# A convolution head and a state-space head on one core: 31 tasks of a written order put elsewhere

## The chip, the cores and the metric

The kernel runs on one core of one Trainium2 chip. The metric is the device time of one execution in microseconds. The median of three runs of the kernel before is 351.68 us (350.0 to 353.27).

## The reference

Two independent computations over 2048 time steps and 1024 channels are put side by side in the output. Inputs and output are bfloat16.

```python
# part A: a gated long convolution
k_shift = sum_t k_pad[:, t:t+S] * shift_k[:, ks-1-t]        # 4 taps along time
kv = k_shift * v
y = irfft(rfft(kv, 2S) * rfft(ssm_k, 2S))[:S]               # per channel, along time
a = q * (y + kv * ssm_D)
# part B: a diagonal complex state-space layer
Lam_bar = exp(dt * Lam);  B_bar = ((Lam_bar - 1) / Lam)[:, None] * Bmat
h_t = Lam_bar * h_{t-1} + x_t @ B_bar.T                     # for t in 0..2047
b = 2 * real(h @ Cmat.T) + x * Dskip
out = concatenate([a, b], -1)
```

## The kernel before, in words

Part A does its transform of length 4096 as 128 times 32 with matmuls. Three arrays in DRAM carry it from stage to stage: `Ys_kv` (first stage of kv), `Ys_h` (first stage of the filter) and `Vs` (after the product). Part B goes over 16 chunks of 128 time steps; a real rotation before and after lets the vector engine's scan do the complex recurrence.

Nothing is scheduled by the machine. The string `ORDER` lists 1489 tasks, and the program calls them in that order (`manual_schedule`, line 766). Each engine and each issuing queue runs its own instructions strictly in that order, and an instruction that waits holds up all that stand behind it on its engine. A task is written `name.arguments:slots`. Slots are chosen by hand: `a` a unit of the on-chip arena of 53 units (2 KB per partition each), `p` one of 8 PSUM banks, `w` one of three slots for transform weights, `h` one of three slots for a chunk's state. A slot that is still in use makes the task wait.

The tasks that matter here, by engine:

- SP issues loads, and a DMA that waits blocks the queue: `x.i` (line 447) a transposing load of chunk i of x, 256 KB; `lh.i` and `lk.i` (676) 512 KB from `Ys_h` and `Ys_kv`, i from 0 to 15; `lw.i` (671) 160 KB of transform weights; `swp.i.q` (707) an exchange on the chip, 256 KB, which copies the even or odd partitions of a tile to the others; `vl.n` (741) 512 KB from `Vs`; `qp.r` (746) 512 KB of q; `osp`, `ysp`, `ysh` stores of the output. `kp.r` (570 to 573) loads rows of k into a ring of eight.
- POOL issues `sw.i.q`, the same exchange from its own queue; `vst.i` (736), 512 KB to `Vs`; `yst.i` (563), `ost.r` (763) stores of the output; `ld_G` (398) a constant.
- PE: `U.i.*` (464), chunk i times B; `yq.i.k` and `y.i.*` (538; 520 and 523), chunk i times C; `sh.g` and `sk.g` (687), second transform stage of filter and kv for group g, two groups to each i; `sa.g` (725), the inverse stage; `a3.n.*` (753), the last stage.
- ACT empties the banks: `ue` (473), `ye` (556), `she` (696), `ske` (703), `sae` (733), `a3e` (760). A `v` at the end of the name (`uev`, `shev`, `a3ev`) puts the same copy on DVE.
- DVE: `r1`, `r2`, `sc`, `r3`, `r4` (487, 498, 504, 510), rotation, scan and rotation of a chunk; `pr.i` (713), the product of the two spectra, which needs both exchanges of i and the evictions of both groups; `qm.r` (762), the gate with q.

So pair i goes: `lw`, `lh`, `lk`, then `sh`/`sk` on PE, `she`/`ske` on ACT, `sw`/`swp`, `pr` on DVE, `sa` on PE, `sae`, `vst`. All sixteen `vst` must land before the first `vl`. The last stage then runs to the end beside the last chunks of part B.

Of the kernel before, what the change touches and what calls it, by code (L numbers as in the profile page):

```python
# [133 lines left out]
sae.1.1:a40 sae.0.0 lw.5:w1 sae.0.1 vst.3 yq.6.4 sh.10:p0p2 yq.6.5 sw.2.0 sh.11:p3p5 yq.6.6 x.14:a36 swp.2.1 sae.1.0  # L134
she.10.1:a0 she.11.1 yq.6.7 sk.4:p1p4 yq.7.0:p5p2 she.10.0 r1.8:a6 ye.6.0:a37 ske.4.0 ye.6.1 ske.4.1 she.11.0 yq.7.1
pr.2 lw.4:w0 cy.8:h2 sh.8:p1p6 sh.9:p0p7 she.9.0:a48 she.8.0 she.9.1 yq.7.2 yq.7.3 sk.11:p0p3 she.8.1 yst.5 sa.5:p7p1
ske.11.1:a4 sae.5.0:a44 sk.10:p4p6 yq.7.4 yq.7.5 lk.4:a28 yq.7.6 lk.6:a21 lh.7:a12 swp.5.0 ske.10.1 sa.4:p3p6 x.11:a14
# [2 lines left out]
sa.11:p6p2 ske.9.1 sae.10.0:a3 U.10.0.0 r4.8 cy.9:h1 sae.10.1 sae.11.0 ue.10.0 U.10.2.0 vst.0 sae.11.1 sw.4.1 ue.10.2  # L140
yq.8.0:p1p0 yq.8.1 lw.6:w2 sh.13:p3p6 yq.8.2 lh.8:a37 lh.11:a1 sh.12:p2p5 r1.9:a40 she.13.0:a27 she.13.1 vst.2 lw.8:w1
yq.8.3 she.12.0 sk.12:p3p7 pr.4 she.12.1 sa.9:p2p6 ske.12.1:a17 lk.8:a9 ske.12.0 sa.8:p4p5 yq.8.4 sae.9.1:a31 swp.6.0
sae.9.0 sae.8.1 r2.9 yq.8.5 sae.8.0 sh.16:p3p7 swp.6.1 vst.5 sk.13:p5p2 she.16.1:a5 she.16.0 yq.8.6 lw.7:w0 lk.7:a46
sh.17:p4p6 yq.8.7 she.17.0 sk.17:p3p7 she.17.1 ske.17.0:a34 sc.9.0 swp.8.1 U.11.0.1:p4 ye.8.1:a3 U.11.0.0 ske.13.0
swp.8.0 ske.17.1 sc.9.1 U.11.3.0:p5 ye.8.0 sh.15:p3p6 sk.16:p0p1 ske.13.1 she.15.1:a37 U.11.3.1 r1.10:a42 sh.14:p2p6
she.15.0 lh.9:a15 sk.15:p7p3 r3.9:a48 ske.16.1 ske.16.0 she.14.0 pr.6 U.11.1.0:p1 lk.9:a22 r4.9 she.14.1 ue.11.3:a12
U.11.1.1 vst.4 skev.15.1:a9 ue.11.0 sa.12:p2p5 ske.15.0 sae.12.1:a32 sa.13:p0p4 U.11.2.0:p7 ue.11.1 yq.9.0:p5p6 cy.10:h2
sw.7.0 sae.13.1 pr.8 sk.14:p4p1 yq.9.1 sae.13.0 ske.14.1 ske.14.0 sae.12.0 sa.16:p3p0 lk.11:a20 r2.10 sae.16.1:a44
sae.16.0 sa.17:p1p4 sae.17.0 sae.17.1 yq.9.2 yq.9.3 sc.10.0 lw.9:w2 sh.19:p1p0 she.19.1:a4 swp.7.1 sh.18:p4p2 vst.8
U.11.2.1 she.18.0 ysp.8 she.19.0 she.18.1 sw.9.0 x.13:a31 lw.11:w1 lh.14:a34 sk.19:p0p3 yq.9.4 ue.11.2 sh.23:p2p1  # L150
she.23.1:a27 lh.15:a43 yq.9.5 sh.22:p4p1 sw.9.1 she.23.0 ske.19.1:a17 she.22.1 she.22.0 yq.9.6 yq.9.7 sk.22:p4p1
ske.19.0 ske.22.0:a15 sk.18:p7p3 ye.9.0:a3 ske.18.1 sc.10.1 r3.10:a46 r4.10 lh.10:a47 ske.18.0 ske.22.1 pr.7
yq.10.0:p0p2 yq.10.1 ye.9.1 pr.9 sk.23:p3p4 yst.7 yq.10.2 ske.23.1 ske.23.0 sa.15:p5p1 yq.10.3 x.12:a52 sa.14:p7p3
lw.10:w0 sae.15.1:a24 sae.15.0 sae.14.0 sa.18:p6p1 sa.19:p5p4 cy.11:h0 yq.10.4 ld_G sae.19.1:a49 sae.18.0 sw.11.0
yq.10.5 yq.10.6 r1.11:a19 r2.11 sae.14.1 sae.19.0 sae.18.1 yq.10.7 sc.11.1 sh.21:p1p3 sh.20:p5p6 yst.9 U.12.1.1:p7
ye.10.0:a42 ye.10.1 shev.21.0:a5 she.20.1 lw.15:w2 lh.12:a1 she.21.1 U.12.1.0 sw.11.1 pr.11 ue.12.1:a22 sc.11.0
r3.11:a17 sh.30:p4p0 sh.31:p2p6 U.12.3.1:p3 she.20.0 she.31.0:a9 sw.10.1 U.12.3.0 lk.10:a45 U.12.0.0:p5 she.30.1
she.31.1 lk.12:a39 she.30.0 ue.12.3 lk.15:a43 swp.10.0 swp.15.0 U.12.0.1 sa.22:p4p3 r4.11 sae.22.0:a37 sa.23:p1p2
U.12.2.0:p6 sae.23.1 sw.15.1 U.12.2.1 uev.12.2 ue.12.0 sae.23.0 sk.20:p0p5 sae.22.1 ske.20.0:a28 sk.21:p7p2 skev.21.0
yq.11.0:p4p1 sk.30:p6p0 ske.20.1 ske.30.1:a18 yq.11.1 sk.31:p3p0 yq.11.2 lw.12:w1 vst.7 lk.14:a47 ske.30.0 ske.31.0  # L160
sh.25:p3p7 yq.11.3 skev.21.1 sh.24:p5p2 ske.31.1 pr.10 she.25.0:a24 sa.20:p0p3 she.25.1 sa.21:p7p6 she.24.1 yq.11.4
she.24.0 vst.11 pr.15 vst.9 sae.20.1:a29 sae.20.0 yq.11.5 r1.12:a2 sk.24:p3p2 sae.21.1 sa.31:p5p0 ysp.10 sae.31.1:a20
saev.31.0 lw.14:w0 yq.11.6 sa.30:p6p0 ske.24.0:a22 sae.30.0 skev.24.1 yq.11.7 saev.21.0 sk.25:p6p5 swp.12.0 sh.28:p7p2
sae.30.1 U.13.3.0:p0 yev.11.1:a28 ye.11.0 sk.29:p1p3 ske.25.1 cy.12:h1 shev.28.1:a16 ske.25.0 sk.28:p2p5 sh.29:p6p4
she.28.0 she.29.0 U.13.3.1 U.13.1.1:p7 r2.12 x.15:a0 ske.28.0:a5 ske.29.0 U.13.1.0 ske.28.1 U.13.2.1:p6 lh.13:a13
ue.13.3:a10 sw.12.1 sc.12.1 lw.13:w2 lk.13:a45 she.29.1 sh.26:p0p4 qp.0:a48 sw.14.1 ske.29.1 she.26.0:a41 sh.27:p5p3
she.27.0 U.13.2.0 pr.12 U.13.0.0:p2 she.27.1 she.26.1 ue.13.2 U.13.0.1 ue.13.1 sk.26:p3p1 swp.14.0 ske.26.0:a1
sk.27:p6p4 sa.25:p7p0 U.15.3.0:p5 ue.13.0 ske.27.1 sae.25.1:a38 sc.12.0 r3.12:a12 U.15.0.1:p2 U.15.3.1 pr.14 U.14.2.1:p3
U.15.0.0 sae.25.0 swp.13.1 ske.27.0 vst.15 ske.26.1 uev.15.3:a50 sw.13.0 sa.29:p7p6 sa.28:p0p1 ue.15.0 sa.24:p4p2 vst.6
ysp.11 sae.29.1:a34 U.15.1.0:p5 sae.24.0 r4.12 sae.24.1 qp.5:a6 vst.10 saev.29.0 sae.28.0 U.15.1.1 U.14.2.0 pr.13  # L170
sa.27:p6p4 ue.15.1 cy.13:h2 sae.28.1 sae.27.0:a8 yq.12.0:p0p7 r1.13:a12 sa.26:p1p2 yq.12.1 yq.12.2 saev.26.0 qp.6:a20
sae.27.1 yq.12.3 U.14.3.1:p5 U.14.1.0:p1 vst.12 sae.26.1 ue.14.2:a24 U.14.0.1:p3 U.14.3.0 vst.14 U.14.1.1 qp.1:a18
U.15.2.0:p4 vst.13 U.14.0.0 ue.14.3 yq.12.4 yq.12.5 ue.14.1 r2.13 sc.13.0 sc.13.1 vl.3:a38 r3.13:a12 r4.13 yq.13.0:p2p1
yq.13.1 yq.13.2 ue.14.0 yq.13.3 r1.14:a40 r2.14:h0 cy.14 vl.13:a44 yq.12.6 vl.1:a16 vl.9:a32 yq.12.7 a3.13.1:p5 sc.14.1
sc.14.0 r3.14:a24 a3e.13.1:a4 vl.2:a2 ye.12.0:a41 U.15.2.1 a3.13.0:p3 a3.1.0:p5 yq.13.4 vl.12:a46 yq.13.5 uev.15.2
yq.13.6 yq.13.7 ye.12.1 a3e.13.0 a3e.1.0:a34 r4.14 r1.15:a22 cy.15:h1 a3.2.1:p4 a3.3.1:p7 vl.6:a8 vl.10:a28 ye.13.0:a11
a3.12.1:p2 a3.12.0:p0 vl.8:a12 r2.15 vl.5:a44 ye.13.1 a3ev.12.0 vl.0:a26 a3.3.0:p3 a3e.2.1:a51 a3ev.3.1 y.14.1.0:p5
qp.4:a46 a3.2.0:p1 a3e.3.0 vl.11:a14 yst.12 a3e.12.1 qm.6 a3e.2.0 y.14.1.1 a3.9.1:p6 y.14.1.2 vl.14:a24 a3.8.1:p1
# [1 line left out]
a3.5.0:p5 a3.9.0:p0 a3.11.1:p7 qm.1 a3ev.9.1:a18 a3.5.1:p6 a3e.8.1 a3e.8.0 a3e.9.0 y.14.0.0:p4 y.14.0.1 osp.6  # L180
a3e.5.1:a12 sc.15.1 a3e.11.1 vl.15:a38 a3.14.1:p1 y.14.0.2 a3e.5.0 a3.10.0:p5 a3e.10.0 sc.15.0 osp.1 r3.15:a42
a3.11.0:p2 a3e.11.0 a3.15.0:p0 a3e.14.1:a14 qm.4 a3.14.0:p7 qm.0 y.14.0.3 a3.6.0:p1 a3ev.14.0 a3.4.0:p7 yst.13 vl.7:a26
qp.2:a20 a3e.6.0:a3 a3.15.1:p3 r4.15 a3e.4.0 a3e.15.0 ye.14.0 ysg.14.0 a3ev.15.1 y.15.1.0:p5 a3.7.0:p2 qp.3:a24 qp.7:a32
y.15.1.1 a3.4.1:p7 qm.5 a3.6.1:p6 qm.7 osp.4 a3e.4.1 a3.7.1:p3 osp.5 y.15.1.2 y.15.1.3 osp.0 a3ev.7.0 ysg.14.1 ost.7
# [657 lines left out]
```

## Time and profile before

| | |
|---|---|
| median of three runs | 351.68 us |
| profiled execution | 352.94 us |
| its span, first to last instruction | 351.0 us |
| PE busy | 332.9 us |
| DVE busy | 326.1 us |
| ACT busy | 273.4 us |
| traffic | 101.09 MB, mean 288 GB/s |

One profiled execution is shown. Its span leaves out what lies before the first and behind the last instruction, so the execution's own time is 1.94 us longer. In a timeline a row gives start, duration, engine, line, operation, and in brackets the idle time of the engine before it and who ended that. A window's row gives each engine's busy time in it, the granted share of PE's clock, the busy share of the 16 DMA engines and the rate. PE's ends are modelled, so a busy PE need not be at its peak.

### The profile page before, as it was taken

The page shows a single profiled execution, that of the slowest core. Times are in us where ns is not written, and L with a number is a line of the kernel's source. Part 1 is how long each engine was busy: PE and PEld are TensorE (multiplying, and loading weights), DVE is VectorE, ACT ScalarE, POOL GpSimd, SP SyncE. Part 2 cuts the span into 40 slices and gives each one's busy share as a digit, 9 for nine tenths or more (in the row PEclk, how much of TensorE's full clock was granted, in tenths as well). Part 3 has the DMA queues.
Part 4 walks back from the last instruction along what each step waited for, and adds up shares of the span by engine and source line. Part 5 has one row for each costly group of instructions (what it writes and reads, how often), then busy time and mean ns, then how long its engine had stood idle before and what let it go on. Part 6 is the DMA issues. An engine that isn't in the chain of part 4 may idle for free. (4 is left out here: it accounts for less than half of the span.)

```text
span 351.0 us, 11815 instructions
## 1 busy us (share of the span) xinstructions
PE 332.9 (95%) x5105; PEld 233.2 (66%) x5105; DVE 326.1 (93%) x261; ACT 273.4 (78%) x524; POOL 68.0 (19%) x110
## 2 busy tenths in 40 slices
...
GB/s 193 357 286 293 278 264 324 271 288 329 279 327 211 319 283 234 324 233 307 308 244 293 194 357 357 309 236 250 292 264 301 288 314 310 229 381 273 366 326 226
DMA packets 62880, 101.09 MB, mean 288 GB/s; under 512 B 29422, under 2 KB 31742, under 8 KB 62828
## 3 DMA queue, kind: packets, MB, share of 16 engines
...
q8 instruction: 40, 0.66, 0.8%
...
## 5 line engine op out<-in xcount | busy, mean ns | idle before, releaser
L464 PEld LDWEIGHTS <-BT 128*128 128x128 bf16 x2048 | 118.4, 99 | 13.7 <-issue 9.2
L464 PE MATMUL bank<-arena,BT 128*128 128x128 bf16 x2048 | 126.0, 221 | 0.3 <-ACT BT L431 0.3
L538 PE MATMUL bank<-CT,gslot 64*64 64x512 bf16 x1408 | 88.2, 378 | 0.1
L504 DVE TENSOR_TENSOR_SCAN gslot<-rtab,gslot 128x1040 bf16<-128x1040 f32 x32 | 72.9, 2310 | 0.7
L538 PEld LDWEIGHTS <-gslot 64*64 64x64 bf16 x1408 | 38.8, 107 | 29.4 <-issue 1.4
L473 ACT CAST arena<-bank 128x512 bf16<-128x512 f32 x61 | 37.2, 642 | 14.0 <-PE bank L464 13.0
L613 ACT CAST arena<-bank 128x512 bf16<-128x512 f32 x64 | 36.6, 658 | 8.0 <-PE bank L607 5.3
L520 PE MATMUL bank<-CT,gslot 128*128 128x512 bf16 x160 | 39.4, 379 | 0.0
L696 ACT CAST arena<-bank 128x512 bf16<-128x512 f32 x62 | 33.4, 615 | 7.3 <-PE bank L687 5.7
L713 DVE TENSOR_TENSOR arena<-arena 128x4096 bf16<-128x4096 bf16 x16 | 36.5, 2285 | 2.3 <-ACT arena L473 1.6
L487 DVE TENSOR_TENSOR arena<-gslot,Z 128x4096 bf16<-128x4096 bf16 x16 | 36.6, 2288 | 0.9 <-PE bank L687 0.4
L703 ACT CAST arena<-bank 128x512 bf16<-128x512 f32 x60 | 33.7, 609 | 4.0 <-PE bank L687 2.6
L487 DVE TENSOR_TENSOR arena<-arena,Z 128x4096 bf16<-128x4096 bf16 x16 | 36.5, 2283 | 0.0
L733 ACT CAST arena<-bank 128x512 bf16<-128x512 f32 x60 | 32.7, 615 | 4.4 <-PE bank L725 4.4
L664 ACT CAST arena<-bank 128x512 bf16<-128x512 f32 x64 | 34.6, 635 | 1.7 <-PE bank L656 1.6
L587 DVE TENSOR_TENSOR arena<-arena 128x4096 bf16<-128x4096 bf16 (+3 forms) x16 | 29.9, 1880 | 0.0
L667 POOL DMA_DIRECT2D Ys_h<-arena x32 | 23.5, 737 | 28.6 <-ACT arena L664 26.1
L616 POOL DMA_DIRECT2D Ys_kv<-arena x16 | 11.1, 711 | 87.2 <-ACT arena L613 86.1
L687 PE MATMUL bank<-arena,wslot 64*64 64x512 bf16 x256 | 22.1, 383 | 4.7 <-DMA wslot<-a_c_W 4.7
L556 ACT CAST arena<-bank 128x512 bf16<-128x512 f32 x31 | 18.3, 601 | 9.9 <-PE bank L523 4.4
L760 ACT CAST arena<-bank 128x512 bf16<-128x512 f32 x26 | 13.6, 600 | 15.6 <-PE bank L753 15.6
L520 PEld LDWEIGHTS <-gslot 128*128 128x128 bf16 x160 | 14.4, 98 | 16.1 <-issue 1.5
...
## 6 DMA issues: line engine op xcount, KB each, us to landing
...
```

Source lines behind the costliest of these rows:

```text
L464: nc.tensor.matmul(pu[:, w, jl, :], BT[:, 2 * jp + jl, w, d, :], xT[:, d, :], start=(d == 0), stop=(d == ND - 1))
L473: cp(st["u", i][:, :, 2 * jp:2 * jp + 2, :], st.pop(("pu", i, jp)))
L487: nc.vector.tensor_mul(m, s_, win(Z))
L504: nc.vector.tensor_tensor_scan(gf, rtab[:].rearrange("p j t -> p (j t)"), gf, 0.0, ALU.mult, ALU.add)
L520: nc.tensor.matmul(py, h[:, w, j, 2:GW], CT[:, j, w, dh * 512:(dh + 1) * 512], start=(j == 0 and w == 0), stop=False)
L538: mm = nc.tensor.matmul(st["py", i, dh][cols, cs(r)], lhs(dh, rows, c), rhs(dh, rows), start=first, stop=last)
L613: cp(st["ysb", n2][:, p, dh * 512:(dh + 1) * 512], st.pop(("pa", n2, p, dh)))
L664: cp(o, st.pop(("pb", hf, s, e, r)).rearrange("p (n c t) -> p n c t", n=2, c=2))
L696: cp(st["hab", i][:, 0, a, l, :], st.pop(("ps", "h", g, l)))
L703: cp(st["x16", i][:, a, l, :], st.pop(("ps", "k", g, l)))
L713: nc.vector.tensor_mul(hab, st.pop(("x16", i)).rearrange("p a l d -> p (a l d)").unsqueeze(1).to_broadcast([P, 2, 2 * D]), hab)
L733: cp(st["vsb", i][:, a, dh * 512:(dh + 1) * 512], st.pop(("pv", g, dh)))
```

## The change

Two things change. In `ORDER` 31 tasks stand elsewhere or in another form; no task is added or dropped. And `kp.-2`, which loads two rows of k into the ring, leaves out the first of them, which no product reads.

The order, word by word, in the stretches that differ (`[-...-]` is taken out there, `{+...+}` put in):

```
yq.6.5 [-sw.2.0-] {+swp.2.0+} sh.11:p3p5 {+lk.4:a28+} yq.6.6 x.14:a36 swp.2.1
...
yq.7.1 {+yq.7.2 yq.7.3+} pr.2 lw.4:w0 cy.8:h2 sh.8:p1p6 [-sh.9:p0p7-] {+sh.9:p4p7+} she.9.0:a48 she.8.0 she.9.1
[-yq.7.2 yq.7.3-] sk.11:p0p3 she.8.1 {+yq.7.4+} yst.5 sa.5:p7p1 ske.11.1:a4 sae.5.0:a44 {+yq.7.5 yst.6+} sk.10:p4p6
[-yq.7.4 yq.7.5 lk.4:a28-] yq.7.6 lk.6:a21 lh.7:a12 swp.5.0 ske.10.1 sa.4:p3p6 [-x.11:a14-] ske.10.0 sw.5.1
...
ue.10.1 [-yst.6-] U.10.2.1:p4
...
ue.10.0 U.10.2.0 {+x.11:a14+} vst.0 sae.11.1 sw.4.1
...
r4.9 [-she.14.1-] ue.11.3:a12 U.11.1.1 vst.4 skev.15.1:a9 ue.11.0 sa.12:p2p5 ske.15.0 {+she.14.1+} sae.12.1:a32
...
swp.7.1 {+x.13:a31+} sh.18:p4p2 vst.8 U.11.2.1 she.18.0 ysp.8 she.19.0 she.18.1 [-sw.9.0 x.13:a31-] {+ld_G+} lw.11:w1
[-lh.14:a34-] {+lh.15:a43+} sk.19:p0p3 yq.9.4 {+yst.7+} ue.11.2 sh.23:p2p1 she.23.1:a27 [-lh.15:a43-] yq.9.5 sh.22:p4p1 sw.9.1
...
r3.10:a46 r4.10 [-lh.10:a47-] {+yq.10.0:p0p2 yq.10.1 yq.10.2 yq.10.3+} ske.18.0 ske.22.1 pr.7 [-yq.10.0:p0p2 yq.10.1-] ye.9.1
[-pr.9-] {+lh.10:a47+} sk.23:p3p4 [-yst.7 yq.10.2-] {+lh.14:a34+} ske.23.1 ske.23.0 sa.15:p5p1 [-yq.10.3-] {+sw.9.0 pr.9+}
x.12:a52 sa.14:p7p3 lw.10:w0
...
yq.10.4 [-ld_G-] sae.19.1:a49
...
sc.11.1 sh.21:p1p3 {+sw.11.1 pr.11+} sh.20:p5p6 yst.9 U.12.1.1:p7 ye.10.0:a42 ye.10.1 shev.21.0:a5 she.20.1 lw.15:w2 lh.12:a1
she.21.1 U.12.1.0 [-sw.11.1 pr.11-] ue.12.1:a22 sc.11.0
...
lk.15:a43 [-swp.10.0-] {+sw.10.0+} swp.15.0
...
U.13.2.1:p6 [-lh.13:a13-] {+lh.13:a7+} ue.13.3:a10
...
yq.13.5 [-uev.15.2-] {+ue.15.2+} yq.13.6
...
a3e.1.0:a34 r4.14 {+vl.11:a14+} r1.15:a22 cy.15:h1 a3.2.1:p4 a3.3.1:p7 vl.6:a8
...
a3e.3.0 [-vl.11:a14-] yst.12
...
y.14.0.1 [-osp.6-] a3e.5.1:a12 sc.15.1 a3e.11.1 vl.15:a38 a3.14.1:p1 [-y.14.0.2-] a3e.5.0 a3.10.0:p5 {+a3.14.0:p7+} a3e.10.0
sc.15.0 osp.1 r3.15:a42 a3.11.0:p2 a3e.11.0 a3.15.0:p0 a3e.14.1:a14 qm.4 [-a3.14.0:p7-] qm.0 {+y.14.0.2+} y.14.0.3 a3.6.0:p1
a3ev.14.0 {+osp.6+} a3.4.0:p7 yst.13
...
osp.0 [-a3ev.7.0-] {+a3e.7.0+} ysg.14.1
```

The load of k:

```diff
         else:
-            spd(t_[1:113, :, :], kr[0:112, 16 + 2 * r:18 + 2 * r, :])
-            spd(t_[113:P, :, :], kr[112:P - 1, 16 + 2 * r:18 + 2 * r, :])
+            o = 1 if r == -2 else 0
+            spd(t_[1:113, o:2, :], kr[0:112, 16 + 2 * r + o:18 + 2 * r, :])
+            spd(t_[113:P, o:2, :], kr[112:P - 1, 16 + 2 * r + o:18 + 2 * r, :])
```

More of the change, by code (lines that the diff above doesn't have):

```diff
@@ L133 @@
 she.4.0 sc.7.0 she.5.1 sk.5:p0p5 sc.7.1 r3.7:a45 sa.0:p1p3 r4.7 lh.4:a50 she.5.0 sa.1:p4p2 ske.5.1:a4 ske.5.0
[L134 to L137, printed above, removed]
+sae.1.1:a40 sae.0.0 lw.5:w1 sae.0.1 vst.3 yq.6.4 sh.10:p0p2 yq.6.5 swp.2.0 sh.11:p3p5 lk.4:a28 yq.6.6 x.14:a36 swp.2.1
@@ L138 @@
+sae.1.0 she.10.1:a0 she.11.1 yq.6.7 sk.4:p1p4 yq.7.0:p5p2 she.10.0 r1.8:a6 ye.6.0:a37 ske.4.0 ye.6.1 ske.4.1 she.11.0
+yq.7.1 yq.7.2 yq.7.3 pr.2 lw.4:w0 cy.8:h2 sh.8:p1p6 sh.9:p4p7 she.9.0:a48 she.8.0 she.9.1 sk.11:p0p3 she.8.1 yq.7.4
+yst.5 sa.5:p7p1 ske.11.1:a4 sae.5.0:a44 yq.7.5 yst.6 sk.10:p4p6 yq.7.6 lk.6:a21 lh.7:a12 swp.5.0 ske.10.1 sa.4:p3p6
 ske.10.0 sw.5.1 sae.5.1 r2.8 sc.8.1 yq.7.7 ske.11.0 sk.8:p0p4 ye.7.0:a11 ske.8.0:a16 sc.8.0 U.10.1.0:p1 pr.5 U.10.0.1:p5
-U.10.1.1 lh.6:a8 sae.4.0 sae.4.1 ske.8.1 ye.7.1 ue.10.1 yst.6 U.10.2.1:p4 sa.10:p7p3 sk.9:p0p1 swp.4.0 r3.8:a32 ske.9.0
@@ L140 @@
[L140 to L178, printed above, removed]
-a3.1.1:p0 a3e.1.1 a3.0.1:p4 y.14.1.3 vl.4:a30 a3e.0.1 ye.14.1:a2 a3.10.1:p3 a3.0.0:p2 a3e.10.1:a22 a3.8.0:p4 a3e.0.0
@@ L180 @@
[L180 to L184, printed above, removed]
@@ L185 @@
-a3e.6.1 a3e.7.1 ye.15.1:a8 qm.3 osp.3 ysh.15.1 qm.2 y.15.0.0:p3 y.15.0.1 y.15.0.2 y.15.0.3 ye.15.0 ysh.15.0 ost.2
+U.10.1.1 lh.6:a8 sae.4.0 sae.4.1 ske.8.1 ye.7.1 ue.10.1 U.10.2.1:p4 sa.10:p7p3 sk.9:p0p1 swp.4.0 r3.8:a32 ske.9.0
+sa.11:p6p2 ske.9.1 sae.10.0:a3 U.10.0.0 r4.8 cy.9:h1 sae.10.1 sae.11.0 ue.10.0 U.10.2.0 x.11:a14 vst.0 sae.11.1 sw.4.1
+ue.10.2 yq.8.0:p1p0 yq.8.1 lw.6:w2 sh.13:p3p6 yq.8.2 lh.8:a37 lh.11:a1 sh.12:p2p5 r1.9:a40 she.13.0:a27 she.13.1 vst.2
+lw.8:w1 yq.8.3 she.12.0 sk.12:p3p7 pr.4 she.12.1 sa.9:p2p6 ske.12.1:a17 lk.8:a9 ske.12.0 sa.8:p4p5 yq.8.4 sae.9.1:a31
@@ new lines @@
+swp.6.0 sae.9.0 sae.8.1 r2.9 yq.8.5 sae.8.0 sh.16:p3p7 swp.6.1 vst.5 sk.13:p5p2 she.16.1:a5 she.16.0 yq.8.6 lw.7:w0
+lk.7:a46 sh.17:p4p6 yq.8.7 she.17.0 sk.17:p3p7 she.17.1 ske.17.0:a34 sc.9.0 swp.8.1 U.11.0.1:p4 ye.8.1:a3 U.11.0.0
+ske.13.0 swp.8.0 ske.17.1 sc.9.1 U.11.3.0:p5 ye.8.0 sh.15:p3p6 sk.16:p0p1 ske.13.1 she.15.1:a37 U.11.3.1 r1.10:a42
+sh.14:p2p6 she.15.0 lh.9:a15 sk.15:p7p3 r3.9:a48 ske.16.1 ske.16.0 she.14.0 pr.6 U.11.1.0:p1 lk.9:a22 r4.9 ue.11.3:a12
+U.11.1.1 vst.4 skev.15.1:a9 ue.11.0 sa.12:p2p5 ske.15.0 she.14.1 sae.12.1:a32 sa.13:p0p4 U.11.2.0:p7 ue.11.1 yq.9.0:p5p6
@@ new lines @@
+cy.10:h2 sw.7.0 sae.13.1 pr.8 sk.14:p4p1 yq.9.1 sae.13.0 ske.14.1 ske.14.0 sae.12.0 sa.16:p3p0 lk.11:a20 r2.10
+sae.16.1:a44 sae.16.0 sa.17:p1p4 sae.17.0 sae.17.1 yq.9.2 yq.9.3 sc.10.0 lw.9:w2 sh.19:p1p0 she.19.1:a4 swp.7.1 x.13:a31
+sh.18:p4p2 vst.8 U.11.2.1 she.18.0 ysp.8 she.19.0 she.18.1 ld_G lw.11:w1 lh.15:a43 sk.19:p0p3 yq.9.4 yst.7 ue.11.2
+sh.23:p2p1 she.23.1:a27 yq.9.5 sh.22:p4p1 sw.9.1 she.23.0 ske.19.1:a17 she.22.1 she.22.0 yq.9.6 yq.9.7 sk.22:p4p1
+ske.19.0 ske.22.0:a15 sk.18:p7p3 ye.9.0:a3 ske.18.1 sc.10.1 r3.10:a46 r4.10 yq.10.0:p0p2 yq.10.1 yq.10.2 yq.10.3
@@ new lines @@
+ske.18.0 ske.22.1 pr.7 ye.9.1 lh.10:a47 sk.23:p3p4 lh.14:a34 ske.23.1 ske.23.0 sa.15:p5p1 sw.9.0 pr.9 x.12:a52
+sa.14:p7p3 lw.10:w0 sae.15.1:a24 sae.15.0 sae.14.0 sa.18:p6p1 sa.19:p5p4 cy.11:h0 yq.10.4 sae.19.1:a49 sae.18.0 sw.11.0
+yq.10.5 yq.10.6 r1.11:a19 r2.11 sae.14.1 sae.19.0 sae.18.1 yq.10.7 sc.11.1 sh.21:p1p3 sw.11.1 pr.11 sh.20:p5p6 yst.9
+U.12.1.1:p7 ye.10.0:a42 ye.10.1 shev.21.0:a5 she.20.1 lw.15:w2 lh.12:a1 she.21.1 U.12.1.0 ue.12.1:a22 sc.11.0 r3.11:a17
+sh.30:p4p0 sh.31:p2p6 U.12.3.1:p3 she.20.0 she.31.0:a9 sw.10.1 U.12.3.0 lk.10:a45 U.12.0.0:p5 she.30.1 she.31.1
@@ new lines @@
+lk.12:a39 she.30.0 ue.12.3 lk.15:a43 sw.10.0 swp.15.0 U.12.0.1 sa.22:p4p3 r4.11 sae.22.0:a37 sa.23:p1p2 U.12.2.0:p6
+sae.23.1 sw.15.1 U.12.2.1 uev.12.2 ue.12.0 sae.23.0 sk.20:p0p5 sae.22.1 ske.20.0:a28 sk.21:p7p2 skev.21.0 yq.11.0:p4p1
+sk.30:p6p0 ske.20.1 ske.30.1:a18 yq.11.1 sk.31:p3p0 yq.11.2 lw.12:w1 vst.7 lk.14:a47 ske.30.0 ske.31.0 sh.25:p3p7
+yq.11.3 skev.21.1 sh.24:p5p2 ske.31.1 pr.10 she.25.0:a24 sa.20:p0p3 she.25.1 sa.21:p7p6 she.24.1 yq.11.4 she.24.0 vst.11
+pr.15 vst.9 sae.20.1:a29 sae.20.0 yq.11.5 r1.12:a2 sk.24:p3p2 sae.21.1 sa.31:p5p0 ysp.10 sae.31.1:a20 saev.31.0 lw.14:w0
```

23 lines of the change are left out of this document (added).

## The prediction

> **What bounds the kernel now.** I read the page first. Its chain of waits is no help: it holds only the last microseconds. The busy line is.
>
> ```profile
> span 351.0 us, 11815 instructions
> ...
> PE 332.9 (95%) x5105; PEld 233.2 (66%) x5105; DVE 326.1 (93%) x261; ACT 273.4 (78%) x524; POOL 68.0 (19%) x110
> ```
>
> Two engines are full, PE and DVE. No matmul is added or dropped, so a moved step gains only by removing a wait of one of these two. Their timelines show the few long waits behind the start. DVE, over the whole span (brackets: idle time before the instruction, and its releaser):
>
> ```profile
> 192.40 2.29 DVE L713 TENSOR_TENSOR arena<-arena 128x4096 bf16<-128x4096 bf16 x1 [0.26 <-ACT arena L703]
> ...
> 209.99 2.29 DVE L713 TENSOR_TENSOR arena<-arena 128x4096 bf16<-128x4096 bf16 x1 [1.61 <-ACT arena L473]
> ...
> 251.26 0.69 DVE L696 CAST arena<-bank 128x512 bf16<-128x512 f32 x1 [2.51 <-PE bank L687]
> ...
> 262.11 0.69 DVE L473 CAST arena<-bank 128x512 bf16<-128x512 f32 x1 [2.13 <-PE bank L464]
> ...
> 339.58 1.23 DVE L762 TENSOR_TENSOR arena<-arena 128x2048 bf16<-128x2048 bf16 x1 [2.82 <-DMA arena<-in_A_q_dram]
> ```
>
> In order these are pr.2, pr.4, shev.21.0, uev.12.2 and qm.7. PE, the same view:
>
> ```profile
> 210.41 0.41 PE L687 MATMUL bank<-arena,wslot 64*64 64x512 bf16 x4 [1.32 <-DMA wslot<-a_c_W]
> ...
> 250.74 0.63 PE L687 MATMUL bank<-arena,wslot 64*64 64x512 bf16 x8 [3.19 <-DMA wslot<-a_c_W]
> 251.30 3.58 PE L464 MATMUL bank<-arena,BT 128*128 128x128 bf16 x32
> ...
> 260.04 1.96 PE L464 MATMUL bank<-arena,BT 128*128 128x128 bf16 x32
> ```
>
> PE waits twice for a weight load: at 210.41 for lw.6, at 250.74 for lw.10. The second wait costs twice: 32 matmuls right behind it take 3.58 us, the same 32 nine microseconds later 1.96, so 1.62 us go to a halved clock. DVE's waits at 251.26 and 262.11 are the same event seen from DVE: both end on PE.
>
> Why do small loads land late? The queue of SP, first the steps before 210, then those before 250:
>
> ```profile
> 180.99 1.94 SPq L447 DMA_TRANSPOSE arena<-in_B_x_dram  x1
> 185.01 0.47 SPq L707 DMA_DIRECT2D arena<-arena  x1
> ...
> 193.41 1.98 SPq L447 DMA_TRANSPOSE arena<-in_B_x_dram  x1
> ...
> 198.83 0.34 SPq L671 DMA_DIRECT2D wslot<-a_c_W  x1
> ```
>
> ```profile
> 231.29 9.39 SPq L676 DMA_DIRECT2D arena<-Ys_h  x3
> 240.78 1.27 SPq L447 DMA_TRANSPOSE arena<-in_B_x_dram  x1
> 243.02 1.32 SPq L671 DMA_DIRECT2D wslot<-a_c_W  x2
> ```
>
> The first are x.14, swp.2.1, x.11, lw.6. lw.6 is issued at 198.83 and awaited until 210.41; lw.10 is issued at 243.02 and awaited until 250.74. Ahead of each stands a transposing load. What such a load does to the traffic (stretch, length, PE, clock, DMA share, GB/s):
>
> ```profile
> 183.00:187.40 4.40, 4.18 (x88) 1.00 1.22 147
> 188.00:196.00 8.00, 7.96 (x176) 1.00 1.00 350
> 196.50:203.00 6.50, 6.38 (x124) 1.00 1.14 122
> 244.40:249.10 4.70, 3.15 (x73) 1.00 1.11 165
> 271.40:272.80 1.40, 1.40 (x36) 1.00 0.91 202
> 316.00:318.00 2.00, 2.00 (x11) 1.00 0.62 154
> ```
>
> I chose the first, third, fourth and fifth stretch by the 256-byte packets of x.14, x.11, x.12 and x.15. Plain loads run at 350 GB/s; while a transposing load is under way the core moves 122 to 165, for 4.4 to 6.5 us. One, x.15, took 1.4. A queue is served in order, so what stands behind a slow one waits. The list of packets behind the page shows one difference: an instruction packet stands in or at the edge of each slow one, none in x.15.
>
> ```profile
> q8 instruction: 40, 0.66, 0.8%
> ```
>
> 40 packets for PE's 10,210 loads and matmuls is one per 255, so these come with PE's own progress, wherever the transposing loads are put.
>
> **The change, first place (182 to 212).** x.11 goes from in front of lh.6, swp.4.0 and lw.6 to a place behind swp.4.0, still in front of lw.6. pr.4 at 209.99 is put down to an eviction that it doesn't read; what it reads and what could come so late is swp.4.0, queued behind x.11. Without x.11 ahead of it 1.61 us of DVE can go. lw.6 keeps x.11 in front, but less stands between: lk.4's 512 KB (1.5 us at 350 GB/s) went ahead of x.14, and yst.6, issued before sw.5.1, no longer holds up lh.8. I expect PE's 1.32 to go. PE can gain no more than that here: **-1.3**. The price is paid by pr.2. swp.2.0 now goes by SP, not POOL, and waits there for the eviction that released swp.2.1 at 185.01. lk.4 and x.14 queue behind it, so x.14 is issued near 186 and swp.2.1 near 188. Its packets began 2.0 us after its issue before (180.99, 183.0), so now at about 188.2, with swp.2.0 and lk.4 (768 KB, 2.2 us from 185.5) just through. pr.2 must have swp.2.1 (256 KB, 0.75 us, and 0.5 allowed for landing) at 192.40, so x.14 may take 2.9 us and costs nothing. By its own row it takes 4.4, which makes pr.2 1.5 late; by x.11's 6.5, 3.6; by x.15's 1.4 nothing. I take under 2.9, as x.14 now falls between two of PE's instruction packets. yq.7.2 to 7.5 move up to keep PE busy while lw.4, queued behind swp.2.1, arrives. sh.9's other bank is free by then. sw.5.1, behind yst.6 on POOL now, starts 0.7 us of data later, but x.11 is out of its way. Bounds of this place: -1.6 (pr.4's whole wait) to +2.0 (3.6 less that 1.6).
>
> **Second place (225 to 262).** she.14.1 goes three evictions later on ACT; the product that needs it, pr.7, stands far behind, and it costs nothing. x.13 passes ysp.8, a store that nobody waits for. lh.15 must wait for vst.8 to land; in front of it stood lh.14, which goes behind lh.10. So lh.14's 512 KB leave a stretch with an empty queue and stand in front of x.12 and lw.10: +1.5 us. Against it: sw.11.1 leaves POOL's place behind yst.9, so its 256 KB no longer share the stretch of x.12, and x.12 starts behind, not on, an instruction packet. If x.12 drops from 4.7 to x.15's 1.4, lw.10 comes 1.8 us sooner; if it takes x.11's 6.5, 3.3 later. I take the middle of 1.4 and 4.7, 3.05: +1.5 - 1.65, about **0**, since no row tells which end is nearer. sw.9.0, behind ld_G and yst.7 now, makes pr.9 up to 0.9 late (320 KB); pr.11 before shev.21.0 fills DVE's wait at 251.26 with 2.29 us of work. Both are hidden: DVE then waits at uev.12.2 for PE anyway, which is bound by lw.10. The four yq.10 ahead of sk.23 and sa.15 are the same PE work in another order. sw.10.0 on POOL and lh.13's slot move waits that end before their users ask.
>
> The skill bears on the 1.62 us. The Trainium skill, "TensorE: Matmul & The Clock Gate", Part 1, says that the clock halves after at least one idle window of about 3.4 us, and that the windows run free of the kernel. The trace agrees in part: 3.19 us of idle halved it, 1.32 did not. By that page a 3.19 us wait would sometimes halve it and sometimes not, and the sum would be 1.6 us lower whenever it did not.
>
> **The tail.** From 250.74 on PE has one gap, the 0.66 us below (a3.15.0, waiting for vl.15). One row each of four timelines, and the time to landing of the two last stores:
>
> ```profile
> 331.67 1.02 PE L753 MATMUL bank<-arena,Gt 128*128 128x512 bf16 x4 [0.66 <-DMA arena<-Vs]
> 332.72 0.36 SPq L746 DMA_DIRECT2D arena<-in_A_q_dram  x1
> 344.02 0.59 ACT L556 CAST arena<-bank 128x512 bf16<-128x512 f32 x1 [3.09 <-PE bank L523]
> 344.43 0.73 POOL L763 DMA_DIRECT2D out_dram<-arena  x1 [2.61 <-issue]
> DMA to landing us min/median/max: 2.9/3.6/4.3
> ```
>
> The 332.72 row is qp.3, held for the slot that a3.14.0 frees; qp.7 stands behind it, and qm.7 waits 2.82 us for qp.7. Now a3.14.0 runs ahead of a3.11.0, a3.15.0 (half a microsecond each by the 331.67 row), the gap and y.14.0.2, so qp.3 is issued near 330. vl.11, ahead of vl.6, fills the 316:318 hole (154 GB/s), which brings later loads about a microsecond forward; osp.6, later on SP, lets vl.15 pass. qm.7's wait and the 0.66 go. uev.15.2 and a3ev.7.0 leave DVE (0.69 each) for ACT, idle there. What is late next is PE: the kernel ends with the later of two landings, ost.2's 344.43 + 4.3 = 348.7 and ysh.15.0's, issued after the 344.02 eviction at 344.6, + 2.9 = 347.5. ost.2 can fall over 2 us; ysh.15.0 falls by 0.66 to 346.9. The end falls by **1.9** (bounds 0, if qp.7 is bound by traffic, to 2.8).
>
> kp.-2 loads half its rows: some 250 KB less, 0.7 us of traffic in a stretch where DVE and PE do not wait: 0, at best -0.7.
>
> **Sum.** -1.3 + 0 - 1.9 = -3.2. The profiled execution took 352.94 (span 351.0), so it would take 349.7; from the median of 351.68, which is 1.3 lower, **348.5**.
>
> **The rivals.** *The clock stays up.* x.12 takes 1.4 us, PE's wait falls by 1.8 to about 1.4, near the 1.32 that did not slow the clock, and 1.62 go too: -1.3 - 1.8 - 1.6 - 1.9 = -6.6, **345.1**. For it speaks x.15; against it, that four of five were slow. The page above allows it with a longer wait as well.
>
> *The first gain is lost.* lw.10 hangs on vst.8 and on traffic, not on PE; what PE gains at 210 it waits longer at 250. Only the tail is left: **349.8**. For it: vst.8's landing, not PE, let the 231.29 row's lh.15 go, and the row stands open for 9.39 us.
>
> *Slower: transposing loads block what is now behind them.* x.14 takes 6.5 us before swp.2.1: pr.2 3.6 late, 2.0 left after pr.4's wait is absorbed; lh.14 adds 1.5 before lw.10; the tail gives 1.9: +1.6, **353.3**. It ends slower once x.14 takes more than 4.9. For it: x.11's row; against: its own 4.4, with an instruction packet inside.
>
> The skill's page "DMA: Bandwidth & Descriptors", under Latency and other measured facts, has a transposing load at 261 GB/s, an estimated 1.0 us for 256 KB. By it this rival could not happen; the rows with 122 to 165 GB/s speak against the page here.
>
> **How the numbers follow.** Less than 1% (3.5 us) is about what a measurement of this kernel can't tell from no change. The forecast gets 0.40, with 1.5 us to either side, so somewhat under half of it (0.17) is beyond 1%; the clock rival 0.24, all faster; the lost gain 0.18, all within 1%; the slower one 0.18, of which 0.07 beyond 355.2. Faster 0.41, same 0.52, slower 0.07. The range 344.6 to 353.0 leaves out some 0.09 below it, of the clock rival, and 0.09 above it, of the slower one.
>
> **What would show it.** Right, if pr.4 and the matmul of lw.6 start without a wait, if PE's wait for lw.10 stays near 3 us, and if qm.7 follows qm.5 at once with ysh.15.0 landing last. Wrong, if pr.2 waits for an exchange, if lw.10's wait is far from 3, or if qp.7 still lands last.

## The result, and the profile after

The changed kernel takes **346.34 us**, the median of six executions (346.0 to 347.77). The kernel before took 351.8 beside it (349.43 to 353.27, six executions). The ratio is 0.9859, 95% interval 0.9815 to 0.9903: faster by 1.4%, 5.5 us. The forecast was 348.5. That lies 2.2 us above the result, and the clock rival, 345.1, lies 1.2 us below it.

The profiled execution took 346.95 us. Its page:

```profile
span 345.2 us, 11815 instructions
...
PE 331.4 (96%) x5105; PEld 232.2 (67%) x5105; DVE 324.7 (94%) x259; ACT 274.8 (80%) x526; POOL 68.0 (20%) x110
```

The long waits of DVE behind 190 us, from its timeline (the columns are those of the timeline before; behind `kp`'s lines, the lines of this kernel are numbered one higher):

```profile
193.35 2.29 DVE L714 TENSOR_TENSOR arena<-arena 128x4096 bf16<-128x4096 bf16 x1 [1.21 <-DMA arena<-arena]
...
240.26 2.29 DVE L714 TENSOR_TENSOR arena<-arena 128x4096 bf16<-128x4096 bf16 x1 [0.88 <-DMA arena<-arena]
...
258.55 0.69 DVE L473 CAST arena<-bank 128x512 bf16<-128x512 f32 x1 [1.51 <-PE bank L464]
...
333.23 1.23 DVE L763 TENSOR_TENSOR arena<-arena 128x2048 bf16<-128x2048 bf16 x1 [0.84 <-DMA arena<-in_A_q_dram]
335.59 2.36 DVE L763 TENSOR_TENSOR arena<-arena 128x2048 bf16<-128x2048 bf16 x2 [1.13 <-ACT arena L761]
```

These are pr.2, pr.9, uev.12.2, qm.7 and qm.3. pr.4's 1.61 us are gone, but pr.2 now waits 1.21 for an exchange. qm.7's 2.82 have become 0.84, and qm.3 waits 1.13 for an eviction, which is new. PE:

```profile
195.00 0.84 PE L538 MATMUL bank<-CT,gslot 64*64 64x512 bf16 x12 [0.47 <-ACT arena L697]
242.41 1.60 PE L726 MATMUL bank<-arena,wslot 64*64 64x512 bf16 x23 [0.54 <-ACT arena L704]
248.81 0.63 PE L688 MATMUL bank<-arena,wslot 64*64 64x512 bf16 x8 [1.22 <-DMA wslot<-a_c_W]
249.37 1.96 PE L464 MATMUL bank<-arena,BT 128*128 128x128 bf16 x32
```

The wait for lw.10 fell from 3.19 to 1.22 us. The 32 matmuls behind it take 1.96 us, not 3.58: the clock stayed up. In front of it are two small waits that were not there before. SP's queue shows why lw.10 came earlier (the first row is lh.15 in the kernel before, the others are the changed kernel):

```profile
239.80 0.37 SPq L676 DMA_DIRECT2D arena<-Ys_h  x1
...
235.01 3.15 SPq L677 DMA_DIRECT2D arena<-Ys_h  x3
238.25 2.40 SPq L447 DMA_TRANSPOSE arena<-in_B_x_dram  x1
243.09 1.30 SPq L672 DMA_DIRECT2D wslot<-a_c_W  x2
```

lh.15 left at 235.01, where it had waited until 239.80 for vst.8, and x.12 at 238.25, where it had been 240.78. lw.10 itself left at the same time as before (243.02), because it takes the slot that sa.14 reads, and sa.14 ended at 243.0. But x.12's data came 1.2 us earlier and took 0.6 us less (window below), and lw.10 landed at 248.76, not near 250.7.

```profile
188.70:192.00 3.30, 3.30 (x79) 2.01 (x73) 3.29 (x2) 2.84 (x7) 0.18 (x1) 1.00 1.27 160
201.40:205.00 3.60, 3.60 (x67) 2.93 (x64) 3.60 (x3) 2.41 (x6) 0.73 (x1) 1.00 1.31 140
...
243.20:247.30 4.10, 4.10 (x95) 2.69 (x87) 3.96 (x3) 3.33 (x8) 0.00 (x0) 1.00 1.25 126
```

These are the stretches of x.14, x.11 and x.12, as in the prediction. To see where the time went in this and the later kernels, I count starts from one instruction of line 602 on DVE (603 in the kernels with the shorter load of k): the first of its last pair, which the timeline shows as `x2`, 4.01 us ahead of the line's very last start in every kernel of the table. It stands ahead of every moved task but `kp.-2`. Every number is read from the traces, in us; "end" is the later of the landings of ost.2 and ysh.15.0.

| kernel | L602's pair, in the span | sh.13 | sa.19 | sh.21 (behind lw.10) | U.12.2.1 | end |
|---|---|---|---|---|---|---|
| before | 147.08 | 63.33 | 96.26 | 103.66 | 113.86 | 201.69 |
| after | 147.08 | 61.85 | 96.31 | 101.73 | 110.30 | 196.18 |
| first_only | 147.50 | 61.81 | 96.58 | 100.59 | 109.17 | 197.22 |
| second_only | 147.06 | 60.99 | 95.03 | 100.79 | 109.37 | 197.72 |
| tail_only | 147.43 | 60.98 | 94.12 | 99.86 | 108.44 | 193.80 |
| tail_lh15 | 147.07 | 60.98 | 93.98 | 98.15 | 106.73 | 192.67 |
| tail_pool | 148.22 | 60.97 | 95.39 | 99.53 | 108.11 | 193.67 |
| x14_behind | 147.08 | 61.65 | 95.37 | 101.30 | 109.88 | 195.37 |
| x12_twice | 147.07 | 61.98 | 96.43 | 105.24 | 116.43 | 202.30 |
| lh14_behind | 148.67 | 61.65 | 96.04 | 100.05 | 108.63 | 194.06 |
| after_lh15 | 147.62 | 61.82 | 96.27 | 100.28 | 108.86 | 194.93 |
| kp_lh15 | 147.13 | 61.93 | 94.74 | 99.24 | 107.82 | 196.34 |
| x12_plain | 147.07 | 60.98 | 94.05 | 99.46 | 108.03 | 195.62 |

The first two rows split the 5.51 us between the two traces. At sh.13 the changed kernel is 1.48 ahead; at sa.19 nothing of that is left, +0.05. At sh.21, -1.93: lw.10's wait. At U.12.2.1, -3.56: the clock adds 1.63. At the end, -5.51: the tail adds 1.95.

One trace is not the kernel, though. Each execution comes with its mean granted clock. Of 69 executions of the kernel before, run beside the experiments, 48 had a mean of 0.992 or less (median 351.55 us) and 21 a higher one (348.73). Traces tie this figure to a halved stretch in the middle: the two that have one, before and x12_twice, have a mean of 0.989, the others 0.993 or more. It is a rough mark, because every trace also has a halved stretch of 1.5 to 6.5 us at its very end. None of the changed kernel's six was below 0.996. The ratios leave out every execution more than 1.5% above its kernel's fastest, which includes some of these; so the experiments below are told by medians and by this count.

### The profile page after: what moved, and what is told of

The parts are those of the page before. It is cut to its first block, busy times and chain, and to the rows that moved or that the text cites. A ratio compares the mean times of both kernels' runs of the same rounds, so it can differ in the third digit from the quotient of the medians.

```text
span 345.2 us, 11815 instructions
## 1 busy us (share of the span) xinstructions
PE 331.4 (96%) x5105; PEld 232.2 (67%) x5105; DVE 324.7 (94%) x259; ACT 274.8 (80%) x526; POOL 68.0 (20%) x110
## 5 line engine op out<-in xcount | busy, mean ns | idle before, releaser
L464 PEld LDWEIGHTS <-BT 128*128 128x128 bf16 x2048 | 116.4, 98 | 13.6 <-issue 9.0
L464 PE MATMUL bank<-arena,BT 128*128 128x128 bf16 x2048 | 123.9, 219 | 0.3 <-ACT BT L431 0.3
L538 PEld LDWEIGHTS <-gslot 64*64 64x64 bf16 x1408 | 39.8, 107 | 29.3 <-issue 1.4
```

What stands on the lines that cost most here:

```text
L464: nc.tensor.matmul(pu[:, w, jl, :], BT[:, 2 * jp + jl, w, d, :], xT[:, d, :], start=(d == 0), stop=(d == ND - 1))
L538: mm = nc.tensor.matmul(st["py", i, dh][cols, cs(r)], lhs(dh, rows, c), rhs(dh, rows), start=first, stop=last)
```

## The experiments

The revised theory: the gain at lw.10 has little to do with PE's progress. SP stands for vst.8's landing at lh.15, x.12 and lw.10 queue behind it, PE waits, and a long wait halves the clock. The rival is the prediction's: each place brings what its own sum said.

### The three places, each alone

**first_only**: all the order's edits between yq.6.5 and yq.8.0.

> The kernel before with the edits of the first place alone (182 to 212 us). The forecast's step: -1.3 us, with lw.6's and pr.4's waits gone. The new theory, read from the trace after (yq.10.7 ends at 247.59 there, 247.55 before, so PE's lead of 1.5 us at sh.13 is gone by then): nothing of it is left at the end by PE, 0 us; what could remain is that vst.8 goes out about 1 us earlier and lets lh.15 and with it lw.10 land earlier, at most -1 us. PE's wait for lw.10 shorter by no more than that, and the half clock still there.

349.68 us (12 executions), before 350.87 (29), ratio 0.9991 (0.9950 to 1.0033). The median is 1.2 lower, but the interval holds no change. Its trace has no wait for lw.10, but PE waits 1.17 at sa.18 for pr.9. The clock was low in 3 of 12, where the kernel before had it low in 23 of 29. So neither side is met in full: the -1.3 is not there as a shift, and what is there is a rarer half clock. Among the executions with the clock up, this kernel's median is 349.35 (9) and the kernel before's, run beside it, 348.17 (6), so without the clock's part it is rather slower.

**second_only**: the edits from yq.8.0 to lk.15, and lh.13's slot.

> The kernel before with the edits of the second place alone (225 to 262 us). The forecast's step: 0 us, PE's wait for lw.10 near 3 us. The new theory: lh.14 behind lh.10 costs x.12 less than the forecast took, lw.10's wait falls to between 1.2 and 2.2 us and the clock stays up behind it: -2.6 to -3.6 us.

348.76 us, ratio 0.9968 (0.9929 to 1.0008); clock low in 3 of 12. In its trace PE waits 1.55 for lw.10 and the clock stays up. The median fell by 2.1, less than the new theory said, and the interval just holds no change. The table shows one cost: sa.19 comes 0.9 us later than in tail_only, which has the old order here.

**tail_only**: the edits from 280 us on.

> The kernel before with the edits of the tail alone (from 280 us on). Both the forecast and the trace after say -1.9 us (a bound of 0 if qp.7 is held by traffic, -2.8 if all of qm.7's wait goes), with the wait for lw.10 and the half clock as before. If the tail gained only because everything ahead of it came earlier: 0.

347.24 us (6 executions), ratio 0.9897 (0.9821 to 0.9972). The six fall apart: 344.92 to 345.81 with the clock at 0.998 or more, 348.67 to 351.52 with 0.990 or less. With the clock up this kernel is faster than the whole change.

These traces also show something about the first place. second_only and tail_only keep its old order, and yet neither shows the two waits on which the first place's -1.3 was built. second_only's timelines:

```profile
208.05 0.39 PE L687 MATMUL bank<-arena,wslot 64*64 64x512 bf16 x4
```

```profile
207.88 2.28 DVE L713 TENSOR_TENSOR arena<-arena 128x4096 bf16<-128x4096 bf16 x1
```

Over all seven traces with the old order, pr.4 waited in one and lw.6's matmul in two (1.32 and 0.76). Without these waits sh.13 stands at 60.98; with the new order, at 61.65 to 61.98.

### What holds lw.10 back

**x12_plain**: the kernel before, with

```diff
+        if i == 12:
+            spd(st[nm, i], x[i * T:(i + 1) * T, :].rearrange("p (d t) -> p d t", d=ND))
+        else:
             nc.sync.dma_start_transpose(st[nm, i], x[i * T:(i + 1) * T, :])
```

> The kernel before, x.12 loaded by a plain load of the same 256 KB in place of a transposing one (so chunk 12 of the second head is computed from untransposed rows). If the transposing load is what holds lw.10 back: 256 KB take 0.75 us at 350 GB/s, not 4.7, lw.10 lands near 246.8 and PE hardly waits; with the clock staying up that is 3.2 + 1.6 less, -4.3 to -4.8 us. If it is the traffic and the instruction packet around it: the plain load takes as long, 0 us, wait near 3 us. Half of the wait gone but the clock still halved: -1.6.

347.74 us, ratio 0.9933 (0.9897 to 0.9970); clock low in 1 of 12. That is 3.1 less than before, where 4.3 to 4.8 was expected from the transposing load's part. In the trace the wait became shorter, but did not go:

```profile
228.39 10.09 SPq L679 DMA_DIRECT2D arena<-Ys_h  x3
238.57 0.42 SPq L448 DMA_DIRECT2D arena<-in_B_x_dram  x1
240.88 1.34 SPq L674 DMA_DIRECT2D wslot<-a_c_W  x2
...
246.53 0.63 PE L690 MATMUL bank<-arena,wslot 64*64 64x512 bf16 x8 [1.19 <-DMA wslot<-a_c_W]
```

The first three rows are SP's, the last PE's. SP still stands for 10 us at the three loads of filter stages, lh.15 among them, and their 1.5 MB are still in front. So the transposing load is at most a part of the wait: tail_only's trace, which has that load and the same order here, waits 1.52. And a wait of this length leaves the clock up in the trace; over the executions it was low in 1 of 12, before in 23 of 29.

**x12_twice**: the changed kernel, and behind the transposing load

```diff
             nc.sync.dma_start_transpose(st[nm, i], x[i * T:(i + 1) * T, :])
+        if i == 12:
+            nc.sync.dma_start_transpose(st[nm, i], x[i * T:(i + 1) * T, :])
```

> The changed kernel with x.12 loaded twice, the second transposing load of the same 256 KB right behind the first: some 2 to 4 us more in front of lw.10 on SP's queue. If the clock halves because PE idles at lw.10: the wait grows from 1.2 to 3 to 5 us, the granted clock falls to 0.991 or less in most executions, and the time is 2 to 4 us for the wait and 1.6 us or more for the clock up, 349.5 to 352. If the clock's fall comes from elsewhere: it stays at 0.996 or more, and the time is 348 to 350, the wait alone.

352.20 us, 5.9 above the changed kernel; clock low in 10 of 12 (0.991 or less in 7). The second load, which writes the same tile, left SP at 247.87, when the first had landed, and lw.10 behind it at 249.81 where it had been 243.09. PE's timeline, and PE's clock (the figure behind the five engines) in a window:

```profile
252.31 1.07 PE L690 MATMUL bank<-arena,wslot 64*64 64x512 bf16 x8 [4.61 <-DMA wslot<-a_c_W]
253.31 3.60 PE L466 MATMUL bank<-arena,BT 128*128 128x128 bf16 x32
```

```profile
251.20:258.00 6.80, 5.69 (x50) 3.87 (x51) 4.90 (x3) 2.13 (x5) 0.00 (x0) 0.50 0.82 276
```

The wait grew by 3.4 us, and the clock was halved for twice the 3.41 us of the trace before. So PE's idle time at lw.10 is what halves the clock. The wait alone would have given some 349.7, so the clock is worth some 2.5 us here; the table has 2.6 (from sh.21 to U.12.2.1 11.19 against 8.57).

**before_lh15**: the kernel before, with one word moved:

```
-... she.23.1:a27 lh.15:a43 yq.9.5 ... x.12:a52 sa.14:p7p3 lw.10:w0 sae.15.1:a24
+... she.23.1:a27 yq.9.5 ... x.12:a52 sa.14:p7p3 lw.10:w0 lh.15:a43 sae.15.1:a24
```

> The kernel before with one edit: lh.15 behind lw.10. If the wait for lw.10 and its half clock are what makes the kernel before slow: no wait, granted clock 0.994 or more in at least 10 of 12 executions, 346 to 347 us, 4 us or so less than before. The tail's own gain is then this kernel's time less 343.57: the forecast says 1.9, the runs of before and of the tail alone with the clock up say 3.

346.74 us (12 executions), before 350.72, ratio 0.9885 (0.9852 to 0.9919); the clock was 0.993 or more in all 12. One load moved behind another brings 4.0 us, where the whole change (32 words of the order, counted in its listing, and the shorter load) brought 5.5. PE's timeline has no wait for lw.10. (Its profiled execution, at 350.04, lost some 4.6 us ahead of the very last start of line 602 and is left out of the table; counted from 4.01 us ahead of that start it has 60.98, 93.98, 98.00, 106.55 and 194.34.)

### What the other places cost

**tail_lh15**: the tail's edits and the same move of lh.15, nothing else.

> The kernel with the tail's edits alone, and lh.15 moved from in front of lh.10 and x.12 to behind lw.10, so that SP no longer stands from 231 to 239 us for vst.8's landing ahead of them. If lw.10's wait (1.5 to 3.2 us) and the half clock behind it hang on lh.15's wait for vst.8: x.12's data are through before lw.10 is issued near 241 to 243, PE's wait for lw.10 is under 0.5 us, the granted clock is 0.994 or more in at least 10 of 12 executions, and the median is 343.5 to 345. If x.12 or the traffic alone sets lw.10's landing: a wait of 1.5 or more as in tail_only, a clock of 0.991 or less in half of the executions, median near 347.

**343.57 us** (342.89 to 345.28, six executions), ratio 0.9798 (0.9756 to 0.9840), clock at 0.996 or more in all six. This beats both kernels: its slowest execution is below the changed kernel's fastest. SP and, in the second fence, PE:

```profile
228.78 7.50 SPq L676 DMA_DIRECT2D arena<-Ys_h  x2
236.38 1.53 SPq L447 DMA_TRANSPOSE arena<-in_B_x_dram  x1
240.86 0.34 SPq L671 DMA_DIRECT2D wslot<-a_c_W  x1
241.38 0.36 SPq L676 DMA_DIRECT2D arena<-Ys_h  x1
```

```profile
244.85 0.39 PE L538 MATMUL bank<-CT,gslot 64*64 64x512 bf16 x4
245.22 0.63 PE L687 MATMUL bank<-arena,wslot 64*64 64x512 bf16 x8
```

**after_lh15**: the changed kernel with `lh.15:a43 lh.14:a34` behind `lw.10:w0`.

> The changed kernel with both lh.15 and lh.14 behind lw.10. PE's wait for lw.10 is then gone, as in the tail's kernel with lh.15 behind lw.10, which took 343.57 us. If the first and second place cost nothing but that wait: 343.3 to 344.0. If they have a price of their own (pr.2's wait for x.14, sa.14's 0.54 us for the later sk.23): 344.5 to 345.5.

346.62 us (344.82 to 347.44), ratio 0.9897 (0.9855 to 0.9940); no wait for lw.10, clock up in all six. With the same repair and the same tail as tail_lh15, the order of the first and second place takes 3.0 us more by the medians and 2.3 us more by the table (194.93 against 192.67). I had expected 1 to 2. At sa.19 the table has 96.27 against 93.98: the loss is complete there. Against the changed kernel the trace gains 1.25 us, and the medians show nothing of it.

**lh14_behind**: the changed kernel with `lh.14:a34` behind `lw.10:w0`.

> The changed kernel with lh.14 moved from in front of x.12 to behind lw.10. By the forecast's price (512 KB, +1.5 us in front of x.12 and lw.10) PE's wait for lw.10 falls from 1.2 to 1.7 us to below 0.4, and the median falls by about 1.2, to 345.1. If x.12 is slow for its own reasons and lh.14's traffic is hidden beside it: the wait stays at 1 or more and the median stays within 0.4 us of 346.3.

346.34 us (344.86 to 347.81), ratio 0.9886 (0.9847 to 0.9925). In the trace the wait for lw.10 is gone and sh.21 stands 1.7 us earlier, as the price of +1.5 said. The median did not move. Its L602 came 1.6 us later in the profiled execution than the changed kernel's, and the intervals of the ratios overlap; so the times can't decide. In the trace x.12's own packets also took less, 2.3 us for 4.1. Two other traces fit the price: first_only and tail_pool issue vst.8 as early, keep lh.14 at its old place, and have no wait for lw.10 either.

**x14_behind**: the changed kernel with `x.14:a36` behind `lw.4:w0`.

> The changed kernel with x.14 moved behind lw.4 on SP's queue, so that nothing but lk.4 stands between swp.2.0 and swp.2.1. If pr.2's wait (1.21 us after the change, 0.26 before) is x.14's doing and is still there at the end: pr.2's wait goes, pr.4 starts 0.8 to 1.2 us earlier, and the median falls by 0.5 to 1.0 to 345.3 to 345.8. If it is taken up by PE's wait for lw.10: pr.2's wait goes and the end stays within 0.3 us of 346.3.

347.10 us (346.20 to 348.61), not lower. pr.2's wait is gone in the trace, so it was x.14's doing. But sh.13 moved by only 0.2, and PE waited 1.72 for lw.10 instead of 1.22. In the trace PE was 0.94 us ahead at sa.19 and 0.43 behind the wait for lw.10, so about half of what was won there was waited away; the medians show no gain.

**tail_pool**: the tail alone, with `sw.2.0` taken out and `swp.2.0` put behind `swp.2.1`.

> The kernel with the tail's edits alone, and one exchange, sw.2.0, issued by SP behind swp.2.1 instead of by POOL. POOL then issues one transfer fewer ahead of vst.8. In five traces POOL's 69th issue (counted from the first) came 1.3 to 3.6 us after what it waited for; it was vst.8 in all three kernels where sw.2.0 is POOL's, and the one behind vst.8 in both where it isn't. If the delay hangs on the count: vst.8 is issued 0.3 us after sae.17.1 instead of 1.83, it lands about 1.5 us earlier, lh.15 with it, lw.10's wait is shorter than tail_only's 1.5, and the clock stays at 0.994 or more in at least 8 of 12; median 345 to 346. If the delay is vst.8's own: still 1.8, median as tail_only, 347.

349.23 us, ratio 0.9940 (0.9893 to 0.9987); clock low in 6 of 12, where at most 4 were expected. POOL's timeline in tail_only, then in this kernel:

```profile
231.93 0.73 POOL L736 DMA_DIRECT2D Vs<-arena  x1 [8.51 <-ACT arena L696]
232.70 1.13 POOL L707 DMA_DIRECT2D arena<-arena  x2
```

```profile
231.17 0.72 POOL L736 DMA_DIRECT2D Vs<-arena  x1 [6.97 <-DMA arena<-in_B_x_dram]
235.01 1.14 POOL L707 DMA_DIRECT2D arena<-arena  x2 [3.11 <-ACT arena L696]
```

vst.8 left 0.30 us behind sae.17.1, not 1.83, as expected. But the delay passed to the next transfer, the exchange sw.9.0; pr.9 then waited 1.61 and PE 1.25 at sa.18. What was won on one side was lost on the other. Which wait halved the clock in six executions the one trace, with its clock up, can't show.

**kp_lh15**: before_lh15 with the shorter load of k.

> The kernel before with lh.15 behind lw.10 and the shorter load of k's first rows as well. The forecast says 0, at best -0.7 us, against the kernel without the shorter load; if less traffic in front of the first rows moves the whole first stage, -0.5 or more shows at the end.

345.14 us (344.76 to 347.34), ratio 0.9872 (0.9831 to 0.9913), against before_lh15's 346.74 (344.27 to 350.04) and 0.9885 (0.9852 to 0.9919). The medians differ by 1.6 us, the ratios hardly, and the ranges overlap. Whether the shorter load brings something stays open.

## Why the prediction was right and wrong

**What bounds the kernel.** Right in the main: most of the time moved where PE or DVE had waited, and from lw.10 to the end PE set the pace. The reading failed in one respect. It took the waits of one trace for the kernel's own. The table and the counts above show two that are chances (lw.6, pr.4) and one whose length varies from run to run (lw.10).

**First place, -1.3: this step failed.** The waits of lw.6 and pr.4 went, as the marks asked, and between the two profiled executions sh.13 came 1.48 us earlier. But six of seven traces of the old order lack pr.4's and five lack lw.6's. Against a trace without them the new order has sh.13 0.85 us later. The price at pr.2 was also set too low: x.14 took 3.3 us where "under 2.9" was free, and pr.2 waited 1.21. That mark, "wrong, if pr.2 waits for an exchange", was hit, though removing this wait in x14_behind did not lower the median. A 0.47 us wait of PE at yq.7.4, for the eviction she.9.0, is part of the 0.85; for the rest I have no row. One thing stays open: the profiled execution of the kernel before has both the waits near 210 us and the long one at lw.10, and tail_only's, with the same order up to 280 us, has neither (1.52 at lw.10, clock up). Whether the first bring the second was not tried.

**Second place, 0: this step failed by more, in the other direction.** Between the two traces it is -1.98 for the wait and -1.63 for the clock. The price of lh.14 held in lh14_behind's trace. x.12 was taken at 3.05 us and took 4.1, so the step was even too kind there. What it left out was vst.8, here in the kernel before (its row in the changed kernel stands in the last section):

```profile
233.87 0.73 POOL L736 DMA_DIRECT2D Vs<-arena  x1 [8.43 <-ACT arena L696]
DMA to landing us min/median/max: 5.4/5.4/5.4
```

It landed at 234.55 and not at 239.25, by three parts: PE and ACT were 1.0 us earlier (sae.17.1 ended at 231.03, before at 232.04), POOL's delay of 1.53 us fell behind it, and it took 3.2 us from issue to landing, not 5.4. The prediction had vst.8 only in a rival, as a reason against a gain. And the edit that lets vst.8 go earlier belongs to the first place: it is swp.2.0 on SP, as first_only and tail_pool show (0.30 us behind sae.17.1 in both, no wait for lw.10 in their traces; over tail_pool's executions the clock was still low in 6 of 12, so that edit alone is not the whole cure). The second place's lh.14 then takes a part back. So the 3.6 us were won at the second place, but not by its edits alone. Two "hidden" edits were not free either: sa.14 waits 0.54 us for the eviction of sk.23, which went behind two yq.10, and in second_only sa.19 is 0.9 us late. From sh.13 to sa.19 the changed kernel takes 1.46 us more than tail_lh15; 1.03 of them fall on sa.14 and sa.18.

**Tail, -1.9: about right.** The two profiled executions give 1.95. Over all traces in the table, U.12.2.1 to the end takes 85.4 to 86.1 us with the new tail (eight kernels) and 87.6 to 88.5 with the old (five), so about 2.4. By the medians of before_lh15 and tail_lh15 it is 3.2, which is beyond the bound of 2.8 that the prediction set. qm.7 does not follow qm.5 at once, as the marks wanted: 0.84 us remain, and qm.3 then waits for ACT. The end is set by ysh.15.0 (343.26) with ost.2 just ahead (342.93), as said.

**kp.-2, 0:** not settled.

**The rivals.** The clock rival's condition, a wait near 1.4 us with the clock up, came true, but not by a shorter x.12. *The first gain is lost* came true in its size: yq.10.7 ends at 247.59, before at 247.55, so nothing of PE's 1.5 us lead at sh.13 reached lw.10. Its mechanism did not: the lead was not waited away at lw.10, it was gone by sa.19, ahead of it. A kept clock, a lost lead and the tail are together the result. The slower rival fell: x.14 stayed below the 4.9 us at which it decides.

So that the number was within its range is luck: two errors of opposite sign went into it, a 1.3 that was not there and a 3.6 that the sum did not hold (the clock rival had 3.4 of it, by a shorter x.12). The later runs give the sum by medians: the repaired wait and clock 4.0 (before_lh15), the tail 2.4 by the traces or 3.2 by the medians (before_lh15 less tail_lh15), and 2.3 to 3.0 given back by the first and second place (after_lh15). That makes -3.4 to -4.9, against -5.5 beside the kernel before and -4.3 to -4.5 against its medians in the later runs (350.60 to 350.87), so the parts fit only to about 1 us. The change bought a steady clock with PE time; one moved load buys it without that price (sa.19 at 93.98 in tail_lh15, 96.31 in the changed kernel).

The page on which the clock rival leaned, the Trainium skill's "TensorE: Matmul & The Clock Gate", Part 1, has the clock halve after an idle window of about 3.4 us. The runs fit that roughly: halved stretches of 3.41 and 6.83 us behind waits of 3.19 and 4.61, and none behind waits of 1.19 to 1.72. The 3.19 is a little less than that window; where between 1.72 and 3.19 the limit lies was not tried.
